# A second product of gate factors, moved in front of the scores of a unit

## The chip, the cores and the metric

The kernel runs on one core of one Trainium2 chip. The metric is the device time of one execution in microseconds (us); the median of three runs is 523.07 us, the lowest 521.63 and the highest 526.06. Unless a unit is named, times are microseconds from the start of the profiled execution's span.

## The reference, cut to what matters

The input goes through a gated linear attention with exponential gates and then through a mixture of experts. For each step `t` of each of 4 x 8 sequences (768 steps, 40 wide):

```
m_new  = max(f + m, i)
f_stab = exp(f + m - m_new);  i_stab = exp(i - m_new)
C = f_stab * C + i_stab * outer(v, k);   n = f_stab * n + i_stab * k
y = sigmoid(o_gate) * (C q) / max(|n q|, 1)
```

The 3072 rows of `y` (320 wide) are then routed: logits plus a softplus-scaled noise, the best two of 8 experts for each row, and for each expert `relu(x w1) w2` weighted and added into the output.

## The kernel before, in words

The steps are cut into chunks of 64. A *unit* is one chunk of two of the four batches, that is 128 rows, with all 8 heads; there are 24 units. A written-out loop (`while i < NU - LEAD`, L792) runs 22 iterations, 0 to 21; each handles parts of several units, since the parts of one unit are spread over successive iterations. The instructions of each engine run in the order in which the loop issues them; no planner reorders them, and every engine waits only for the data and the buffers that its next instruction needs.

What an iteration `i` puts on the engines, in the order of the code:

- **k_part, p_part** (VectorE): the keys and the scores of unit `i+1` are multiplied by its gate factors `W` (L350, L356).
- **c_part, o_part** (TensorE): the state update of unit `i` into the bank `st` (L370), its copies on ScalarE (L373), and the output of unit `i` into the bank `o` (L379).
- **e_part** (TensorE, then ScalarE): the *gate factors* of unit `i+2`. A product of 98 rows and 512 columns (L318) gives the exponents of one of the two batches; ScalarE takes their exponential into `W` (L321). `p` = 0 is the first product, `p` = 1 the second. Both go into the one bank named `e`, so that the second product has to wait until the exponential of the first has read the bank.
- **f_part** (VectorE, GpSimd): normalizes the output of unit `i` and multiplies it with the sigmoid of its output gate (L384 to L391).
- **l_part, r_part, b_part** (TensorE): router logits of unit `i-2` (L422), in some iterations ranks (L431 to L433) or a *burst* of products that builds the table of rows (L442).
- **t_part, tc_part**: transposes of unit `i-1` on TensorE (L402), their copy on ScalarE (L406). **lc_part, bc_part** copy logits, ranks and burst out of the bank (L471, L474, L451).
- **s_part** (TensorE): the scores of unit `i+2`, 8 products of 64 x 64 x 256 (L339) and 32 of 64 x 64 x 64 (L342), which work in quarters of the array.
- **sig_part** (ScalarE): the sigmoid of the output gate of unit `i+1`, three instructions in place (L326 to L328).
- **act** issues small exponentials and logarithms of the router on ScalarE when they are due (L685); **fill** issues router work on VectorE up to a budget.

In even iterations from 8 on, ScalarE and GpSimd also split a piece of the first expert's weights (L150). The weights, queries and values arrive over DMA queues that the SyncE engine issues; GpSimd issues the writes of the finished rows. After the loop the last two units are finished by hand, and the experts follow, from about 126 us to the end.

Of the kernel before, what the change touches and what calls it, by code (L numbers as in the profile page):

```python
# [41 lines left out]
LEAD = 2  # L42
# [19 lines left out]
def build(ctx, tc, qk, vk, fi, noise, wgn, w1, w2, cst, ce, out):  # L62
# [59 lines left out]
    def piece_w1(e, f, k):  # L122
        c = slice(f, f + 512)
        if k < 2:
            SP.dma_start(RAW1[:, k, c], w1[e, 128 * k:128 * k + 128, c])
        else:
            for p in range(2):
                SP.dma_start(RAW1[64 * p:64 * p + 64, 2, c], w1[e, 256:320, c])
# [25 lines left out]
    def load_unit(u, what="kv", q=None):  # L154
        pr, c = divmod(u, NCH)
        if "k" in what:
            for n in (slice(0, 32), slice(32, D)):
                for p in range(2):
                    (q or SP).dma_start(QK[u % 4][64 * p + n.start:64 * p + n.stop], qk[pr, c, p, n])
        if "v" in what:  # L160
            flat = VKS[u % 4].rearrange("p x c -> p (x c)")
            SP.dma_start(flat[0:64, 0:VW], vk[pr, c, 0])
            SP.dma_start(flat[64:128, 648:648 + VW], vk[pr, c, 1])
# [59 lines left out]
    def gate_move(kk, q=(SP, SP)):  # L223
        pr, k = divmod(kk, GB)
        j = kk % 2
        src = HL[32 * pr:32 * pr + 32, :, k * GC * L:(k + 1) * GC * L].bitcast(F32)
        q[0].dma_start(LE[j][64:96, :, 64:128].bitcast(F32), src[:, 0].rearrange("r (c t) -> r c t", c=GC))
        q[1].dma_start(RE[j][96:98].bitcast(F32), src[:, 1])
# [43 lines left out]
    def gate_steps(n):  # L272
        for _ in range(n):
            next(gates2, None)
# [9 lines left out]
    def constants():  # L284
        P.memset(W1L[0:64, 2].bitcast(F32), 0.0)
        P.memset(zrow, 0.0)
        P.memset(TBL, 0.0)
        P.memset(WTS, 0.0)
# [23 lines left out]
    def e_part(u, ps_=(0, 1), first=False):  # L312
        pr, c = divmod(u, NCH)
        j = (GB * pr + c // GC) % 2
        c = c % GC
        for p in ps_:
            ps = XTB if first and p else psum.tile([128, 512], F32, name="e")
            T.matmul(ps, LE[j][0:KE, c, 64 - 64 * p:192 - 64 * p], RE[j][0:KE, p, :, c * L:c * L + L], start=True, stop=True)  # L318
            if p == 0:
                W[u] = wk.tile([128, 2, H, L], F32, name="w", bufs=LEAD)  # L320
            A.activation(W[u][:, p].rearrange("p h t -> p (h t)"), ps, AF.Exp)  # L321

    def sig_part(u):

        g = SG[u % 4]
        A.activation(g, g, AF.Exp, scale=-1.0)  # L326
        A.activation(g, g, AF.Ln, bias=1.0)
        A.activation(g, g, AF.Exp, scale=-1.0)  # L328
# [4 lines left out]
    def s_part(u):  # L333
        q = QK[u % 4]
        for h in range(H):
            if whole(u) and h % 4 == 0:
                for p in range(2):
                    r = qrow[p]
                    T.matmul(SQ[u][:, p][r][:, h:h + 4, :], ident[r, r], q[r, 0, h:h + 4, :], start=True, stop=True)  # L339
            for p in range(2):  # L340
                r = qrow[p]
                T.matmul(SQ[u][:, p][half[p], h, :], q[r, 1, h, :], q[r, 0, h, :], start=True, stop=True)  # L342

    def whole(u):
        return u % NCH > 0

    def k_part(u):
        if u % NCH < NCH - 1:
            KD[u] = wk.tile([128, 2, H, D], F32, name="kd")
            V.tensor_mul(KD[u], VKS[u % 4][:, :, 328:648].rearrange("p x (h d) -> p x h d", h=H),  # L350
                         W[u][:, :, :, L - 1:L].to_broadcast([128, 2, H, D]))

    def p_part(u):
        PP[u] = wk.tile([128, 2, H, L], F32, name="p")
        if whole(u):
            V.tensor_mul(PP[u], SQ[u], W[u])  # L356
        else:
            for p in range(2):
                n = half[p]
                V.tensor_mul(PP[u][n, p], SQ[u][n, p], W[u][n, p])  # L360
# [32 lines left out]
    def keep_rows(u):  # L393
        (P if u < XV - 1 else SP).dma_start(XD[128 * u:128 * u + 128, 0:DM], XR[u])
# [50 lines left out]
    def bc_part(t, b, late=False):  # L445
        if b:
            s = late or rt.tile([128, NE * TC], F32, name="share", bufs=2)
            if late:
                V.tensor_add(TBL, TBL, t[:, LGC + 24:LGC + 24 + NE * TC])
            else:  # L450
                A.activation(s, t[:, LGC + 24:LGC + 24 + NE * TC], AF.Copy)  # L451
                P.tensor_add(TBL, TBL, s)
            done[0] += len(b[0]) // 2

    def decode(a, b):

        t, n = TBL[:, a:b], slice(a, b)
        V.scalar_tensor_tensor(VC[:, n], t, 0.0, cs[:, C_VAC + a:C_VAC + b], op0=OP.is_equal, op1=OP.mult)
        V.tensor_scalar(AB[:, n], t.bitcast(I32), 16, 0x7fff, op0=OP.arith_shift_right, op1=OP.bitwise_and)
        V.tensor_scalar(KM[:, n, 0], t, 0.0, None, op0=OP.is_gt)  # L460
        V.scalar_tensor_tensor(TOK[:, n], AB[:, n], -float(CODE), VC[:, n], op0=OP.add, op1=OP.add)
        V.tensor_scalar(KM[:, n, 1], t, 0.0, None, op0=OP.is_lt)
# [282 lines left out]
    def gather(e, h=None, ts=None):  # L745

        for t in ts or tiles(e, h):

            n = NTOK if h is None else 128 * E0U[h]
            P.indirect_dma_start(out=XG[0:rows_of(e, t), t], out_offset=None, in_=XD[0:n],  # L750
                                 in_offset=bass.IndirectOffsetOnAxis(ap=token(e, t), axis=0),
                                 bounds_check=n - 1, oob_is_err=False)
# [3 lines left out]
    def early_w2(j, n):  # L756

        SP.dma_start(raw2[:, j:j + n], w2[0, 128 * j:128 * (j + n)].rearrange("(j p) c -> p j c", p=128))
# [8 lines left out]
    def tiles(e, h=None):  # L767
        if h is None:
            return range(6 + (CAPS[e] > NM))
        c = parts(e)[h]  # L770
        return range(c.start // 128, -(-c.stop // 128))
# [19 lines left out]
    i = 0  # L791
    while i < NU - LEAD:  # L792
        unit[0] = i
        spent[0] = 0.0
        while sent:
            SP.dma_start(*sent.pop())
        if 1 <= i and i + 3 < NU:
            load_unit(i + 3)
        if i:
            keep_rows(i - 1)  # L800
        if i % 2 == 0 and i and i // 2 + 2 < 2 * GB:
            gate_move(i // 2 + 2, (P, P) if i < XV else (SP, SP))

        if W1LD <= i < W1LD + 12 and i % 2 == 0:
            j = (i - W1LD) // 2
            piece_w1(0, 512 * (j // 3), j % 3)
        if i == W2AT:
            early_w2(0, 2)
        if i == 3:
            SP.dma_start(cs[:, C_TRI:], cst[:, C_TRI:])  # L810
        if i == 4:
            SP.dma_start(nzt, noise)
        if not begun and done[0] >= E0U[0]:
            decode(0, E0S[1] // 128)
            spent[0] += 0.6
            begun = 1
        if begun and late < len(tiles(0, 0)):
            gather(0, 0, tiles(0, 0)[late:late + 2])
            late += 2
            begun = 2  # L820
        if i == 6:
            constants()
            A.activation(tri, cs[:, C_TRI:C_TRI + 128], AF.Copy)
            A.activation(ones, cs[:, C_ONE:C_ONE + 128], AF.Copy)
            A.activation(iob, cs[:, C_N:C_N + 128], AF.Copy)
        k_part(i + 1)
        p_part(i + 1)
        fill(0.2, False)
        s_room(i + 2)
        c_part(i)  # L830
        o_room(i)
        o_part(i)
        e_part(i + LEAD, (0,))
        if i == 0:
            sig_part(0)
        f_part(i, lambda: fill(0.15, False))
        if i < 2:
            gate_steps(4)
        if i == 0:
            gate_move(2, (P, P))  # L840
        t = l_part(i)
        w = r_part(t)
        b = None if w else b_part(t)
        if i:
            t_part(i - 1)
            tc_part(i - 1)
        lc_part(i, t, w)
        bc_part(t, b)
        s_part(i + 2)
        act()  # L850
        if i:
            sig_part(i + 1)
        e_part(i + LEAD, (1,))
        if i == 0:
            sig_part(1)
        route(i)
        fill((SHARE if i < NU - 3 else 0.8) - spent[0])
        if W1AT <= i < W1AT + 12 and i % 2 == 0:
            next(pre1)
        act()  # L860
        if 0 < i < 7:
            gate_steps(4)
        if 6 <= i < 13:
            P.memset(XG[:, i - 6], 0.0)
        i += 1
# [482 lines left out]
```

## Time and profile before

| | before |
|---|---|
| median of three runs | 523.07 us |
| profiled execution, its own time | 522.65 us |
| span of the profiled execution | 520.9 us |
| TensorE busy, share of the span | 504.6 us, 97% |
| VectorE, ScalarE, GpSimd busy | 341.3, 248.7, 243.3 us |
| mean granted TensorE clock | 0.985 |

The profile shows one execution. PE is the matmul side of TensorE, PEld its weight loads, DVE is VectorE, ACT is ScalarE, POOL is GpSimd, SP is SyncE. A row of a timeline gives the start, the duration, the engine, the line, the operation and the tiles written and read; a number in brackets at its end is the idle time of the engine ahead of it and what ended that. Rows with a count merge several instructions. Durations of matmuls contain their way through the array, so that the spacing of their starts, not their duration, says what they cost the engine.

### The profile page before, as it was taken

Reading aid. Unit: us, or ns where it says so; the run is one execution under the profiler, and the core shown is the slowest. Engines: PE = TensorE matmul, PEld = TensorE weight load, DVE = VectorE, ACT = ScalarE, POOL = GpSimd, SP = SyncE. Lnnn points to the kernel's source line nnn. Section 1 sums busy time; section 2 is a strip of 40 time slices with the busy share of each in tenths; the row PEclk is TensorE's granted clock in tenths of the full one; section 3 lists DMA queues with packets and bytes.
Section 4 is the critical chain, followed back from the end, with each engine's and each line's share of the span. In section 5 each row is a group of like instructions: output and inputs, shape, how many; then the busy total and the mean of one; then the engine's idle time right before and its main releaser. Section 6 shows DMA issues by size and latency. Waiting matters only on the chain.

```text
span 520.9 us, 13365 instructions
## 1 busy us (share of the span) xinstructions
PE 504.6 (97%) x5130; PEld 473.3 (91%) x5130; DVE 341.3 (66%) x905; ACT 248.7 (48%) x594; POOL 243.3 (47%) x321
## 2 busy tenths in 40 slices
PE   8899999999999999999999999999999999999993
PEld 3788888888889988999999999999999999999993
DVE  6899998986997576763865484377548347546310
ACT  5788879978523255441542354054335325515300
POOL 7545686864543846055415614550562254151033
PEclk9799999999989999999999999999999999999998
DMA  5889999986655848079229516832951683272033
GB/s 153 201 217 243 246 242 248 223 235 207 216 195 165 202 57 213 5 163 234 68 53 274 112 28 139 229 91 48 263 99 51 138 221 88 60 169 26 2 40 41
DMA packets 48955, 76.89 MB, mean 148 GB/s; under 512 B 10645, under 2 KB 37980, under 8 KB 48884
## 3 DMA queue, kind: packets, MB, share of 16 engines
q1 hardware_dynamic: 35668, 52.19, 36.3%
q0 software_dynamic: 11616, 20.57, 20.7%
q10 hardware_dynamic: 1600, 3.21, 2.0%
q8 instruction: 42, 0.69, 0.6%
q14 instruction: 29, 0.24, 0.2%
HBM read 52.42 MB, written 17.40 MB: 134 GB/s over the span
## 4 chain that ended last, share of the span: by engine, by line
PE 66%; DMA 13%; DVE 11%; ACT 3%; issue 2%; POOL 2%; SPq 1%; POOLq 0%; DVEq 0%; ACTq 0%
PE s L981 16%; DMA y_out<-y,tok 9%; PE e L981 8%; PE o L1009 4%; PE o L1008 4%; PE o L1007 4%; PE st L1008 4%; PE st L1009 4%; PE st L1007 4%; PE o L379 4%; PE e L318 3%; PE s L342 2%; DVE hlo L993 2%; PE st L370 2%; DMA qk<-qk_in 2%
## 5 line engine op out<-in xcount | busy, mean ns | idle before, releaser
L1035 POOL DMA_INDIRECT y_out<-y,tok x53 | 87.2, 1645 | 184.8 <-DVE y L1025 182.0
L992 ACT ACTIVATE hh<-s 128x384 fp32r<-128x384 f32 (+3 forms) x91 | 42.6, 470 | 83.8 <-PE s L981 82.7
L981 PE MATMUL s<-xh,w1h 128*128 128x384 f32 (+6 forms) x273 | 76.8, 337 | 0.1
L750 POOL DMA_INDIRECT xg<-rows,tok x53 | 57.3, 1082 | 24.6 <-issue 15.5
L993 DVE SCALAR_TENSOR_TENSOR hlo<-s,hh 128x384 fp32r<-128x384 f32 (+3 forms) x91 | 47.6, 523 | 24.9 <-ACT hh L992 24.3
L981 PE MATMUL s<-xh,w1l 128*128 128x384 f32 (+6 forms) x273 | 61.7, 334 | 0.0
L1009 PE MATMUL o<-w2h,hlo 128*128 128x320 f32 x184 | 56.9, 309 | 0.7 <-DVE hlo L993 0.7
L1008 PE MATMUL o<-w2l,hh 128*128 128x320 f32 x184 | 56.8, 309 | 0.0
L1007 PE MATMUL o<-w2h,hh 128*128 128x320 f32 x184 | 56.3, 306 | 0.2 <-ACT hh L992 0.2
L1009 PE MATMUL st<-w2h,hlo 128*128 128x320 f32 x168 | 51.9, 309 | 0.0
L1008 PE MATMUL st<-w2l,hh 128*128 128x320 f32 x168 | 51.8, 308 | 0.0
L1007 PE MATMUL st<-w2h,hh 128*128 128x320 f32 x168 | 51.2, 305 | 0.0
L981 PEld LDWEIGHTS s<-xh,w1h 128*128 128x128 f32 x273 | 49.2, 188 | 1.5 <-ACT xh L782 0.4
L981 PEld LDWEIGHTS s<-xh,w1l 128*128 128x128 f32 x273 | 47.7, 188 | 1.1 <-DVE xh L784 0.2
L981 PE MATMUL s<-xl,w1h 128*128 128x384 f32 (+6 forms) x182 | 46.1, 334 | 0.3 <-DVE xl L783 0.3
L992 ACT ACTIVATE hh<-e 128x384 fp32r<-128x384 f32 (+3 forms) x45 | 21.3, 473 | 49.3 <-PE e L981 49.3
L981 PE MATMUL e<-xh,w1h 128*128 128x384 f32 (+6 forms) x135 | 38.6, 340 | 0.6 <-DVE hlo L993 0.3
L1025 DVE TENSOR_SCALAR y<-o,gw 128x320 f32<-128x320 f32 x22 | 12.1, 550 | 39.9 <-PE o L1009 39.9
L391 POOL TENSOR_TENSOR xr<-tm,vk 128x320 f32<-128x320 f32 x24 | 21.1, 879 | 34.7 <-DVE tm L390 13.6
L1025 DVE TENSOR_SCALAR y<-st,gw 128x320 f32<-128x320 f32 x20 | 11.0, 550 | 39.3 <-PE st L1009 39.3
L1009 PEld LDWEIGHTS o<-w2h,hlo 128*128 128x128 f32 x184 | 34.5, 188 | 0.9 <-DVE hlo L993 0.9
L1007 PEld LDWEIGHTS o<-w2h,hh 128*128 128x128 f32 x184 | 34.5, 188 | 0.6 <-ACT hh L992 0.4
(237 smaller groups left out, 1290.7 us busy)
## 6 DMA issues: line engine op xcount, KB each, us to landing
vk<-vk_in SPq DMA_DIRECT2D x48, 242.0 KB
raw<-w_in SPq DMA_DIRECT2D x6, 1280.0 KB
raw<-w_in SPq DMA_DIRECT2D x6, 1024.0 KB
qk<-qk_in SPq DMA_DIRECT2D x46, 128.0 KB
y_out<-zrow SPq DMA_DIRECT2D x15, 320.0 KB
raw<-w_in SPq DMA_DIRECT2D x16, 256.0 KB
rows<-xr POOLq DMA_DIRECT2D x23, 160.0 KB, 4.3
xt__2801<-xb SPq DMA_DIRECT2D x40, 72.0 KB
```

Of the source, the lines that this page charges most:

```text
L318: T.matmul(ps, LE[j][0:KE, c, 64 - 64 * p:192 - 64 * p], RE[j][0:KE, p, :, c * L:c * L + L], start=True, stop=True)
L379: T.matmul(OQ[u][half[p], h, :], PP[u][n, p, h, :], VK[u % 4][p][n, h * 41:h * 41 + 41], start=True, stop=True)
L391: P.tensor_mul(XR[u], tm.rearrange("p h d -> p (h d)"), SG[u % 4])
L750: P.indirect_dma_start(out=XG[0:rows_of(e, t), t], out_offset=None, in_=XD[0:n], in_offset=bass.IndirectOffsetOnAxis(ap=token(e, t), axis= ...
L981: T.matmul(ps[:, 0:n], l, r, start=i == 0, stop=i == len(ops) - 1)
L992: A.activation(hi, x, AF.Relu)
L993: V.scalar_tensor_tensor(lo, x, 0.0, hi.bitcast(F32), op0=OP.max, op1=OP.subtract)
L1007: T.matmul(ps, HH[:, j, c], W2H[:, j], start=j == 0, stop=False)
L1008: T.matmul(ps, HH[:, j, c], W2L[:, j], start=False, stop=False)
L1009: T.matmul(ps, HLO[:, j, c], W2H[:, j], start=False, stop=j == 7)
L1025: V.tensor_scalar(y[0:n], ps[0:n], GW[e][0:n, t:t + 1], None, op0=OP.mult)
L1035: st = P.indirect_dma_start(out=out, out_offset=bass.IndirectOffsetOnAxis(ap=token(e, t), axis=0), in_=y[0:n], in_offset=None, compute_op= ...
```

## The change

In iterations 1 to 21 the second product of gate factors of unit `i+2` and its exponential are issued behind the copies of logits and transposes and in front of the scores `s_part`; so the product stands on TensorE between the transposes and the scores, and the exponential on ScalarE in front of `act` and of the three instructions of the sigmoid. In iteration 0 the order stays as it was.

```
         lc_part(i, t, w)
         bc_part(t, b)
+        if i:
+            e_part(i + LEAD, (1,))
         s_part(i + 2)
         act()
-        if i:
-            sig_part(i + 1)
-        e_part(i + LEAD, (1,))
         if i == 0:
-            sig_part(1)
+            e_part(LEAD, (1,))
+        sig_part(i + 1)
         route(i)
```

## Rows read from the trace of the kernel before

**Rows 1.** Windows view, stretches 27 to 48 and 79 to 113 us: busy us by engine, clock, DMA.

```profile
27.00:48.00 21.00, 20.88 (x526) 18.15 (x527) 19.78 (x42) 17.52 (x43) 8.57 (x14) 1.00 0.88 226
79.00:113.00 34.00, 33.47 (x817) 28.92 (x816) 30.12 (x90) 29.92 (x76) 24.22 (x37) 1.00 0.95 234
```

**Rows 2.** Timeline of TensorE's matmuls, iteration 13 of the loop (start us, us).

```profile
81.42 0.50 PE L318 MATMUL e<-re,le 98*128 98x512 f32 x1
81.75 0.74 PE L422 MATMUL xt<-wgt,xts 128*128 128x16 f32 x6
82.34 0.53 PE L402 MATMUL xt<-cs,xr 128*128 128x128 f32 x3
82.80 0.43 PE L339 MATMUL s<-qk,cs 64*64 64x256 f32 x2
...
83.89 0.51 PE L318 MATMUL e<-re,le 98*128 98x512 f32 x1
84.33 0.82 PE L370 MATMUL st<-vk,kd 104*40 104x41 f32 x32
...
86.01 0.49 PE L318 MATMUL e<-re,le 98*128 98x512 f32 x1
```

**Rows 3.** Timeline of TensorE: transposes with a whole-array product behind them.

```profile
129.95 0.52 PE L402 MATMUL xt<-cs,xr 128*128 128x128 f32 x3
130.23 0.60 PE L981 MATMUL s<-xh,w1h 128*128 128x384 f32 x2
```

**Rows 4.** Timeline of TensorE, iteration 0, a stretch at half clock.

```profile
19.22 0.79 PE L318 MATMUL e<-re,le 98*128 98x512 f32 x1
19.94 0.69 PE L339 MATMUL s<-qk,cs 64*64 64x256 f32 x2
...
21.86 0.79 PE L318 MATMUL e<-re,le 98*128 98x512 f32 x1
22.58 1.32 PE L370 MATMUL st<-vk,kd 104*40 104x41 f32 x32
```

**Rows 5.** Timeline of ScalarE, iteration 13.

```profile
81.95 0.60 ACT L321 ACTIVATE w<-e 128x512 f32<-128x512 f32 x1
82.91 0.49 ACT L406 ACTIVATE xts<-xt 128x384 f32<-128x384 f32 x1 [0.35 <-PE xt L402]
...
84.74 0.58 ACT L321 ACTIVATE w<-e 128x512 f32<-128x512 f32 x1
```

**Rows 6.** Timeline, all engines: a product of factors that waited for its bank.

```profile
69.85 0.58 ACT L321 ACTIVATE w<-e 128x512 f32<-128x512 f32 x1
...
70.48 0.19 PEld L318 LDWEIGHTS e<-re,le 98*128 98x128 f32 x1 [0.16 <-ACT w L321]
```

**Rows 7.** Timelines of TensorE and ScalarE: late first exponentials, iterations 8 and 14.

```profile
57.18 0.50 PE L318 MATMUL e<-re,le 98*128 98x512 f32 x1
...
58.00 0.58 ACT L321 ACTIVATE w<-e 128x512 f32<-128x512 f32 x1
...
86.81 0.58 ACT L321 ACTIVATE w<-e 128x512 f32<-128x512 f32 x1
```

**Rows 8.** Timelines of TensorE and ScalarE, iteration 1.

```profile
25.31 0.49 PE L402 MATMUL xt<-cs,xr 128*128 128x128 f32 x3
...
25.50 0.60 ACT L321 ACTIVATE w<-e 128x512 f32<-128x512 f32 x1
```

**Rows 9.** Timeline of VectorE, iterations 3 and 4.

```profile
34.33 0.79 DVE L350 TENSOR_TENSOR kd<-vk,w 128x640 f32<-128x640 f32 x1
...
39.06 0.81 DVE L350 TENSOR_TENSOR kd<-vk,w 128x640 f32<-128x640 f32 x1
```

**Rows 10.** Waits between engines, 17 to 126 us (total us, times, longest us).

```profile
DVE kd L350 <- ACT w L321: 5.1, 5, 2.4
```

**Rows 11.** Timelines of VectorE and TensorE: the burst of iteration 18.

```profile
103.19 2.87 DVE L615 TENSOR_SCALAR ob<-iob,bi,cs 128x128 bf16<-128x128 bf16 x10
...
105.41 0.91 PE L442 MATMUL xt<-oa,ob 128*128 128x56 bf16 x12
```

## The prediction

> **What bounds the kernel now.** I first read the windows view. In the loop TensorE is busy without a gap that matters, 33.47 of 34.00 us between 79 and 113 us, at the full granted clock of 1.00; VectorE (30.12), ScalarE (29.92) and the DMA engines (share 0.95) are close behind it. Between 27 and 48 us VectorE is nearer to full than later (19.78 of 21.00) [rows 1]. A busy matmul row does not say what is lost between two kinds of products, so I read TensorE's timeline next, by the spacing of starts. Iteration 13 takes 86.01 - 81.42 = 4.59 us from first product of factors to first product [rows 2]. In it the transposes stand for 0.46 us before the scores start (82.80 - 82.34), and the second product for 0.44 before the state update starts (84.33 - 83.89), while the first, with the logits behind it, stands for only 0.33 (81.75 - 81.42) [rows 2]. The difference is what follows: a product in pieces of the array (scores, state) costs its predecessor more than one that uses the whole array. The same three transposes with a whole-array product behind them take 130.23 - 129.95 = 0.28 us [rows 3].
>
> So the change, which only reorders, does touch TensorE's path: it takes away one passage from whole-array work to scores (the transposes') and turns the passage scores to product to state into product to scores to state.
>
> **The change part by part, TensorE.** Nothing is added or removed; the 21 products, 21 exponentials and 63 sigmoid instructions of iterations 1 to 21 stay, and the moved step issues no DMA.
>
> Transposes to product: 0.28 instead of 0.46, so -0.18 us. Product to scores: not in the trace at full clock. At half clock, product to scores is 19.94 - 19.22 = 0.72 and product to state 22.58 - 21.86 = 0.72, equal [rows 4], so I take the 0.44 that product to state costs now: no difference. Scores to state: nowhere in the trace. Now scores to product is 83.89 - 82.80 = 1.09 [rows 2]. It may cost more by the 0.11 that a passage to pieces costs over one to whole-array work (0.44 - 0.33), and less by at most the 0.19 of a whole weight load of the product [rows 6]. I take 1.09, since the 40 score products in it are the same, and keep -0.19 and +0.11 for the range. Sum for an undisturbed iteration: 0.28 + 0.44 + 1.09 = 1.81 against 0.46 + 1.09 + 0.44 = 1.99, or -0.18 us.
>
> **The new wait.** The second product needs the bank that the first exponential reads, and now it comes 0.28 us after the transposes' start instead of behind the scores. In iteration 13 the exponential runs from 81.95 to 82.55 [rows 5]; a product that waits for its bank starts its load 0.05 us after the exponential's end (69.85 + 0.58 = 70.43, load at 70.48) [rows 6]. So it could start at 82.60, and TensorE reaches it at 82.34 + 0.28 = 82.62, or 1.20 after the first product. There is no slack, but no loss. What queues behind a late one is everything on TensorE: the scores and the next state update.
>
> ScalarE is late in some iterations, behind splits and router exponentials. In iteration 8 the product could start at 58.00 + 0.58 + 0.05 = 58.63, TensorE would be there at 57.18 + 1.20 = 58.38: 0.25 late, a net of +0.07. In iteration 14 it is 86.81 + 0.63 = 87.44 against 87.21: 0.23 late, net +0.05 [rows 2, 7]. These are the two worst that I saw among iterations 7 to 21; three more (9, 15, 17) lie between them and iteration 13, and I count them at the middle, -0.06 each. The other ten are clean. Iterations 7 to 21: 10 x 0.18 + 3 x 0.06 - 0.07 - 0.05 = 1.86 us gained.
>
> Iteration 1 has no logits, which brings the product closer to its predecessor: it could start at 25.50 + 0.60 + 0.05 = 26.15, and TensorE is there at 25.31 + 0.28 = 25.59 [rows 8]. The wait of 0.56 less 0.18 costs 0.38. That is hidden, and so is any gain of iterations 2 to 6: there VectorE, with its gate steps, sets a period of 39.06 - 34.33 = 4.73 us [rows 9] against TensorE's 4.59, which leaves TensorE 5 x 0.14 = 0.7 us. If VectorE did not pace those, the 0.38 would show and five more gains of 0.18 with it. I count both at nothing.
>
> **ScalarE and VectorE.** In iteration 13 the second exponential goes from 84.74 to behind the copy of the transposes, which ends at 82.91 + 0.49 = 83.40 [rows 5]: 1.3 us earlier. By then its product (82.62, with a duration of 0.51) is done, so ScalarE does not wait. The sigmoid moves back by the one exponential's 0.6 us; GpSimd uses it only an iteration later, so nothing follows. Who gains is VectorE, which stood 5.1 us in five places for that exponential [rows 10]. It is not the bound there, so those 5.1 us are no gain by themselves; they let VectorE run ahead of the two bursts. That matters, because the burst of iteration 18 ends at 105.41 + 0.91 = 106.32, shortly behind VectorE's last operand at 103.19 + 2.87 = 106.06 [rows 11]. What TensorE gains in iterations 13 to 17 (0.18 - 0.05 + 0.06 + 0.18 + 0.06 = 0.43), and in 7 to 11 ahead of the first burst (0.18 - 0.07 + 0.06 + 0.18 + 0.18 = 0.53), survives only if VectorE is earlier too. I keep half of this 0.96.
>
> **Sum.** 1.86 - 0.48 = 1.4 us, carried to the end, since the experts' part is TensorE's. Against the profiled execution, 522.65 - 1.4 = 521.25; that execution is 0.42 under the median of 523.07, so on the scale of the runs 521.7.
>
> **The rivals.**
>
> *No change: another engine paces the loop.* VectorE at 30.12 and the DMA engines at 0.95 of 34 us [rows 1] leave little to follow with, and any earlier TensorE then waits at a burst or for a load. For it: rows 11; against it: TensorE's own 33.47. Time 523.1.
>
> *Slower: ScalarE's lag decides.* ScalarE is busy 29.92 of 34 us and stands a further 0.35 us in each iteration until the transposes are done [rows 1, 5]; at 34 / 4.59 = 7.4 iterations that is 2.6, together 32.5. Gaining 0.18 per iteration leaves 34 - 1.3 = 32.7, so it is about full, and its first exponential may slip in every iteration as it does in 8 and 14. The place is the bank of the two products; the point is a first exponential that starts more than 0.53 + 0.18 = 0.71 us after its product (0.53 is iteration 13's). With twice the lag of iteration 8 in all fifteen, 15 x (0.50 - 0.18) = 4.8 us, 527.9; with half as much again, 15 x (0.38 - 0.18) = 3.0, 526.1. [...] Against it: lags push themselves out, since a TensorE that waits gives ScalarE time. I put it at 525.5.
>
> *Faster than forecast: the product's weights are in place before it may start.* In the row that shows a product waiting for its bank, the load itself started after the exponential, 0.19 us long [rows 6]. Were it done under the transposes, up to 0.19 more would go in each of fifteen iterations: 2.9 on top of 1.86, 518.3. The same size would come from a cheap passage from scores to state (the -0.19 above). [...]
>
> **How the numbers follow.** Forecast 0.50, no change 0.27, slower 0.15, faster still 0.08. The time is the forecast's, 521.7. Its own bounds are wide: scores to state at +0.11 in fifteen iterations is +1.65, which turns it into no change; at -0.19 it is the third rival; and three runs of one kernel spread from 521.63 to 526.06. The range 519.4 to 524.4 holds most of the first two cases and some of each of the others, about 8 in 10. A measurement can tell about 1%, 5.2 us, from no change. Faster than 517.8 needs the third rival and the gains of iterations 2 to 6 on top: 0.04. Slower than 528.3 needs more than the dear end of the second: 0.03. Within: 0.93.
>
> **What would show it.** Right: transposes to second product about 0.28, product to scores about 0.44, scores to state about 1.1; an undisturbed iteration of 4.4 us; VectorE's waits for the second exponential far below 5.1 us; the loop ending 1 to 2 us earlier. Wrong: weight loads of the second product idle behind the first exponential by more than 0.2 us in most iterations (slower), or a loop that ends when it did, with TensorE waiting for VectorE or loads instead (no change).

## The result and the profile after

| | before | after |
|---|---|---|
| median of 19 runs each, same chip | 522.87 us (519.93 to 526.45) | 527.37 us (522.17 to 532.94) |
| ratio | | 1.0067, 95% interval 1.0042 to 1.0092 |
| profiled execution, its own time | 522.65 us | 523.21 us |
| span; TensorE busy | 520.9; 504.6 us | 521.3; 499.0 us |

The kernel became 0.67% slower, about 3.5 us. I had forecast 521.7 and nothing above 524.4. The profiled execution of after is one of the fastest of its 19 runs, so the pair of profiles differs by 0.6 us where the medians differ by 4.5: most of the loss has to be looked for in further executions, as is done below. The ratio, unlike the medians, leaves out three runs of after (530.1 to 532.9 us) as disturbed. The 0.6 us are there when the experts begin: their first product starts at 130.82 us, against 130.23 before [rows 3], and from there to the end it is 390.5 and 390.7 us.

The windows view of after, the same stretches as [rows 1] (columns: TensorE matmul, weight loads, VectorE, ScalarE, GpSimd busy us; granted clock; DMA share; GB/s):

```profile
27.00:48.00 21.00, 18.66 (x398) 16.41 (x396) 19.54 (x40) 14.16 (x34) 8.63 (x13) 0.89 0.95 234
79.00:113.00 34.00, 33.40 (x838) 29.62 (x837) 31.37 (x90) 29.66 (x75) 23.98 (x37) 1.00 0.96 242
```

In the second stretch after runs 838 matmuls where before ran 817, at the same busy time: here the new order is faster. In the first it ran 398 against 526, and the granted clock is 0.89.

The timeline of TensorE, iteration 13, to be laid beside [rows 2]:

```profile
83.73 0.50 PE L318 MATMUL e<-re,le 98*128 98x512 f32 x1
84.07 0.74 PE L422 MATMUL xt<-wgt,xts 128*128 128x16 f32 x6
84.65 0.52 PE L402 MATMUL xt<-cs,xr 128*128 128x128 f32 x3
84.93 0.48 PE L318 MATMUL e<-re,le 98*128 98x512 f32 x1
85.35 0.43 PE L339 MATMUL s<-qk,cs 64*64 64x256 f32 x2
...
86.44 0.82 PE L370 MATMUL st<-vk,kd 104*40 104x41 f32 x32
...
88.12 0.49 PE L318 MATMUL e<-re,le 98*128 98x512 f32 x1
```

Transposes to product 0.28, product to scores 0.42, scores to state 1.09, one iteration 4.39 instead of 4.59 us. The waits of other engines on the new place, after, 17 to 126 us (total us, times, longest us):

```profile
PEld e L318 <- ACT w L321: 2.8, 4, 1.6
DVE kd L350 <- ACT w L321: 2.5, 2, 1.4
...
PE o L379 <- issue: 1.9, 1, 1.9
PE e L318 <- ACT w L321: 1.7, 3, 1.3
```

VectorE's stand for the second exponential fell from 5.1 [rows 10] to 2.5 us. So the mechanism of the gain is there. Where the time went shows in the spacing of first products, after and then before:

```profile
18.14 0.50 PE L318 MATMUL e<-re,le 98*128 98x512 f32 x1
...
36.79 0.50 PE L318 MATMUL e<-re,le 98*128 98x512 f32 x1
...
55.37 0.50 PE L318 MATMUL e<-re,le 98*128 98x512 f32 x1
...
121.77 0.50 PE L318 MATMUL e<-re,le 98*128 98x512 f32 x1
```

```profile
38.58 0.50 PE L318 MATMUL e<-re,le 98*128 98x512 f32 x1
...
52.61 0.50 PE L318 MATMUL e<-re,le 98*128 98x512 f32 x1
...
120.64 0.50 PE L318 MATMUL e<-re,le 98*128 98x512 f32 x1
```

These are iterations 0 (after only; before it is 19.22 [rows 4]), 4, 7 and 21. From 0 to 4 after takes 18.65 us against 19.36. That is not the order's doing: before ran from 17.39 to 24.22 us at half clock [rows 4], and after did not; the old order of h1 (below), which like after is at full clock there, takes 18.64 (first products at 17.55 and 36.19). From 7 to 21 it is 66.40 against 68.03, a gain of 1.63 (I had 1.86 less half of 0.96). But from 4 to 7 it takes 18.58 against 14.03: 4.55 us lost in three iterations. TensorE's timeline there, iteration 5, and the windows before and behind the stand:

```profile
40.48 0.90 PE L379 MATMUL o<-vk,p 104*64 104x41 f32 x24 [0.16 <-DVE tm L390]
43.23 0.43 PE L379 MATMUL o<-vk,p 104*64 104x41 f32 x8 [1.86 <-issue]
43.60 0.80 PE L318 MATMUL e<-re,le 98*128 98x512 f32 x1
...
50.98 0.50 PE L318 MATMUL e<-re,le 98*128 98x512 f32 x1
```

```profile
36.00:43.40 7.40, 5.38 (x143) 4.77 (x139) 7.09 (x14) 4.92 (x12) 3.87 (x6) 1.00 1.02 241
43.50:50.30 6.80, 6.80 (x103) 6.10 (x101) 5.33 (x10) 3.98 (x12) 4.02 (x8) 0.50 0.93 248
```

TensorE stands 1.86 us in the middle of 32 like products, and "issue" says that the profile shows no semaphore, no buffer and no other engine that held it. Right behind the stand the granted clock is 0.50 from 43.50 to 50.30 us; the product of factors there takes 0.80 instead of 0.50, and the way from iteration 5's first product to iteration 6's (43.60 to 50.98), in which the profile shows no wait of TensorE's products, 7.38 us instead of the 4.39 from there to iteration 7's (50.98 to 55.37): 2.99 more. The stand's 1.86 and these 2.99, less three gains of 0.19, make 4.3, against the 4.55 lost.

**What the stand is.** The page's table of DMA queues has a row that I had passed over; before and after have it alike:

```profile
q8 instruction: 42, 0.69, 0.6%
```

42 packets of 16,384 bytes each, which I read as TensorE's program arriving while it runs; the page counts them against the same 16 DMA engines as the loads. The trace has 10,402 TensorE instructions, 248 for each packet, and the stands listed here, and every one above 0.6 us that the rows below put down to "issue", come at a TensorE instruction whose number is 193 modulo 256. Counted out of the trace (times in us; "asked" is when TensorE reached the boundary before, since no row shows the request itself):

```
kernel             number  asked   packet           goes on  stand
before              1985    48.19   50.21 -  51.23    53.99   none
before              4801   106.64  109.67 - 110.94   112.52   0.45
before              5313   117.92  121.12 - 122.16   123.68   0.62
after               1473    36.10   40.43 -  41.78    43.23   1.86
after, again (e1)   3777    86.50   92.23 -  93.38    94.95   3.05
after, again (h4)   1729    41.60   44.86 -  45.96    47.47   0.59
after, again (h4)   2241    54.20   57.40 -  58.46    59.88   0.53
```

In the loops of before and after a boundary comes every 4.7 to 6 us where no stand and no half clock lies between. The packet for the next 256 instructions starts after the boundary before; where that takes 1 to 2 us (the first row), it has landed with time to spare. In the other rows it starts 3 us or more late; there TensorE goes on 1.4 to 1.6 us after the packet has landed, and stands until then. A late packet need not cost anything: behind after's stand the next one started 3.6 us late too and had landed at 47.99, but TensorE, at half clock, came to it only at 51.34. While the packet of number 1473 waits the DMA engines are full: share 1.02 in the window above. The kernel before had such stands too, "PE s L342 <- issue: 1.0, 2, 0.6" in its own waits, and I read over it.

### The profile page after: what moved, and what is told of

The parts are those of the page before. It is cut to its first block, busy times and chain, and to the rows that moved or that the text cites. A ratio compares the mean times of both kernels' runs of the same rounds, so it can differ in the third digit from the quotient of the medians.

```text
span 521.3 us, 13367 instructions
## 1 busy us (share of the span) xinstructions
PE 499.0 (96%) x5130; PEld 470.9 (90%) x5130; DVE 343.2 (66%) x905; ACT 248.0 (48%) x594; POOL 242.4 (47%) x321
## 4 chain that ended last, share of the span: by engine, by line
PE 60%; DMA 14%; DVE 11%; ACT 7%; issue 3%; SPq 2%; POOL 1%; POOLq 0%; DVEq 0%; ACTq 0%
PE s L981 16%; DMA y_out<-y,tok 9%; PE e L981 8%; PE o L1009 4%; PE o L1008 4%; PE o L1007 4%; PE st L1009 4%; PE st L1008 4%; PE st L1007 4%; PE o L379 3%; DVE hlo L993 3%; DMA qk<-qk_in 2%; PE e L318 2%; PE s L342 2%; DVE w2l L764 1%
```

## The experiments

Each kernel is timed against the kernel before on the same chip; chips differ (before: 523 to 530 us), so kernels are compared within a group.

**First group: where in the loop does it lose?** The rivals then were waits of the first iterations (EARLY) and ScalarE's lag throughout (LAG). The kernels differ in the one condition under which the new place holds, `i > 0` (e1, the change as it is), `i > 1` (e2), `i > 6` (e3), `0 < i < 7` (e4). e3, against before, cut to the new place:

```
+        moved = i > 6
+        if moved:
+            e_part(i + LEAD, (1,))
...
+        if not moved:
             e_part(i + LEAD, (1,))
```

e1: 

> The changed kernel once more, for a second trace and a time beside the variants. Theory EARLY: the loss is made in iterations 1 to 6, where the second product waits for ScalarE (1.34 us in iteration 1 of the changed kernel's trace) and where a stall of TensorE or a stretch at half clock can follow; iterations 7 to 21 gain 1.5 to 2 us as forecast. It expects a ratio to the kernel before of 1.005 to 1.009, and in the trace a distance from the first product of iteration 7 to that of iteration 21 near 66.4 us, against 68.0 before. Theory LAG: the product waits for a late ScalarE all along the loop; it expects the same ratio, with waits of the product above 0.2 us in most of iterations 7 to 21 and no gain in that distance.

e2: 

> New order from iteration 2 on; iteration 1 keeps the old one. EARLY, if the wait of iteration 1 is the cause: the loss is gone, ratio 0.996 to 1.000. LAG: the loss stays, 1.005 or more. If something else in iterations 2 to 6 is the cause, the loss stays too, and the next run is without it.

e3: 

> New order in iterations 7 to 21 alone. EARLY: ratio 0.996 to 0.999, some 1 to 2 us faster than the kernel before. LAG: 1.004 or more, since most of the waits stay.

e4: 

> New order in iterations 1 to 6 alone. EARLY: the whole loss and none of the gain, ratio 1.008 to 1.012. LAG: a third of the loss at most, 1.000 to 1.003.

Measured against before: e1 531.66 us, 1.0069 [1.0001, 1.0138]; e2 530.08, 1.0045 [0.9978, 1.0111]; e3 531.59, 1.0066 [1.0001, 1.0131]; e4 530.61, 1.0056 [0.9995, 1.0117]. EARLY's 0.996 to 0.999 for e3 lies outside its interval; that either part of the loop alone loses is likely, but the intervals are too wide to show it. The trace of e1 tells what to look for: from iteration 7 to 21 it takes 75.5 us, where EARLY had 66.4, and no second product there waits more than 0.2 us for ScalarE, where LAG had most of them. TensorE's timeline and two windows (the first from boundary to packet, the second behind the stand):

```profile
90.85 1.04 PE L379 MATMUL o<-vk,p 128*64 128x41 f32 x29
94.95 0.31 PE L379 MATMUL o<-vk,p 104*64 104x41 f32 x3 [3.06 <-issue]
```

```profile
86.50:92.20 5.70, 5.21 (x134) 4.44 (x130) 5.55 (x16) 5.37 (x16) 3.37 (x6) 1.00 0.99 264
...
95.20:102.00 6.80, 6.80 (x102) 6.15 (x101) 4.70 (x22) 3.59 (x10) 3.26 (x7) 0.50 0.92 238
```

The same picture as after's iteration 5, in another iteration and larger: for 5.7 us the DMA engines are full at 0.99 and the code packet does not start, TensorE stands 3 us, and the clock is at 0.50 behind it. EARLY and LAG both fall as the main cause, and a third theory takes their place.

**Second group: code packets behind the loads, or the order itself?** FETCH: the stands come from code packets delayed by a full DMA. ORDER: the new order loses by its own waits. f1 (old order) and f2 (new) load less:

```
-        if "v" in what:
+        if "v" in what and u < 4:
```

f1: 

> The old order, with the values, keys and output gates loaded for units 0 to 3 only; later units read the same four buffers again, so about half of the bytes of the loop's loads and none of its engine work is left out. FETCH (TensorE's code comes in 16,384-byte packets over the same loaded DMA engines, and where such a packet starts late TensorE stands; in the new order it stands more often and longer): the code packets start soon after they are asked for, no stand of over 0.3 us at an instruction number of 193 modulo 256 in the loop, 0.5 to 4 us faster than the kernel before (0.992 to 0.999). ORDER (the new order is slower because of its own waits for ScalarE, whatever the loads do): within 0.998 to 1.002 of the kernel before, as no engine's work has changed.

f2: 

> The new order, with the same loads left out as in the run beside it. FETCH: with the loads out of the way the gain of about 0.19 us in each iteration comes through to the end: 1.5 to 3.5 us faster than the old order with these loads left out (ratio between the two 0.993 to 0.997), no long stand at an instruction number of 193 modulo 256, half clock no more often than in the old order. ORDER: it is slower than the old order with these loads left out, by the same 2 to 4 us as with all loads (ratio 1.003 to 1.009).

f3 (new order) doubles a product, f4 (old order) drops one:

```
-            T.matmul(ps, LE[j]..., RE[j]..., start=True, stop=True)
+            for _ in range(1 + (p == 1 and u > LEAD)):
+                T.matmul(ps, LE[j]..., RE[j]..., start=True, stop=True)
```

```
-            for j in range(3):
-                T.matmul(t[:, LGC:LGC + 16], ..., start=(j == 0), stop=(j == 2))
+            for j in range(2):
+                T.matmul(t[:, LGC:LGC + 16], ..., start=(j == 0), stop=(j == 1))
```

f3: 

> The new order, in which from unit 2 on the second product of gate factors is issued twice into the same place (2 instructions and about 0.22 us of TensorE more in each of 18 or so iterations; its exponential starts that much later). FETCH: code is asked for as often in time, since instructions and time grow together; TensorE is nearer to its old pace of 4.6 us an iteration and stands less often, so the time is that of the changed kernel or lower (1.000 to 1.006 of the kernel before). ORDER: 18 times 0.2 us come on top of what the changed kernel lost: 1.010 to 1.016.

f4: 

> The old order, with the third of the three matmuls of the router's logits left out (the logits lack the last columns), which takes 2 to 4 instructions and about 0.19 us off TensorE's part of each iteration, as the new order does, but without touching the order of products, scores and exponentials. FETCH: a TensorE that is faster by this little gains nothing at the end, because it meets its code sooner: 0.998 to 1.008 of the kernel before, with stands and half clock in the loop as in the changed kernel. ORDER: only the new order loses, so this one shows the whole 3 to 4 us (0.992 to 0.995).

Measured: f1 521.41 us, 0.9973 [0.9950, 0.9995]; f2 519.96, 0.9936 [0.9908, 0.9965]; f3 529.58, 1.0122 [1.0077, 1.0167]; f4 522.33, 0.9977 [0.9950, 1.0004].

The pair f1 and f2 is the clearest of the study: with the DMA engines half empty (shares of 0.46 and 0.48) the sign turns, new to old 0.9936 / 0.9973 = 0.9963, by medians 1.45 us faster, about the gain forecast (the interval of that ratio, worked out below, ends at 1.000). The mean clock of their runs is equal, 0.991 and 0.991. From 25 to 125 us, f1 and then f2, and f2's waits of TensorE for ScalarE:

```profile
25.00:125.00 100.00, 98.55 (x2401) 85.33 (x2401) 88.34 (x231) 84.45 (x211) 64.50 (x100) 1.00 0.46 141
```

```profile
25.00:125.00 100.00, 95.81 (x2384) 85.18 (x2382) 90.55 (x234) 84.09 (x210) 64.03 (x102) 1.00 0.48 142
```

```profile
PE e L318 <- ACT w L321: 1.7, 3, 1.3
...
PE s L342 <- issue: 0.9, 1, 0.9
PE o L379 <- issue: 0.8, 1, 0.8
```

f2 has the same 1.7 us of waits for ScalarE as after, and wins. So ScalarE's lag is not what costs, and ORDER falls as the whole cause. The two waits on "issue" are a miss for FETCH, which expected no long stand in f2: they are stands for code, of 0.76 and 0.88 us (numbers 1473 and 4801), behind packets that started 3.4 and 3.8 us late; f1 has none. No half clock follows them. On average over the loop the packets start 0.8 us late in f1, 1.6 in f2, 1.8 in before and 2.0 in after: with half the loads the new order still has its code late. A third packet shows that full DMA engines are not the only reason; it started 3.2 us late (number 1729) while their share was 0.25:

```profile
41.60:44.80 3.20, 3.15 (x63) 2.74 (x64) 3.03 (x7) 1.90 (x5) 0.21 (x1) 1.00 0.25 92
```

But FETCH in the form in which I had put it falls too. It said that TensorE meets its code sooner because it is faster. f3 is back at the old pace (4.63 us in undisturbed iterations) and should have been no slower than after; it came out at 1.0122, where ORDER had it. Its profile, of its slowest run, has the longest stand of all:

```profile
96.39 0.64 PE L380 MATMUL o<-vk,p 128*64 128x41 f32 x15
101.35 0.87 PE L380 MATMUL o<-vk,p 128*64 128x41 f32 x12 [4.33 <-issue]
```

That is number 3777 again, asked at 91.86, its packet from 98.46 to 99.73. Against the order alone (1.0067 to 1.0083) that is 2 to 3 us more, for about 4 us of added work. Its interval is 2.4 us wide to either side, and work in this loop need not show in full at the end (f4, next), so f3 does not tell how much of the loss the slower pace took away; its profile shows that it did not end the stands. f4 makes TensorE faster by as much as the change does (4.37 us in undisturbed iterations), without touching the order of the products. Some 20 x 0.2 = 4 us of work gained 1.2 at the end (0.0023 of 523, 2.6 at most by the interval), a value between both expectations: a gain of TensorE's in this loop is passed on in part. Its profile has the stands that FETCH expected, in the old order: the longest is 1.89 us, at number 5313 (asked at 119.39, packet from 123.70), and behind it 31 products of L379 take 1.93 us, where 32 take 1.13 from 130.56 on.

**Third group: take traffic away or add it, with the result unchanged.** g1 (new order) and g2 (old) load expert 0's first weights as whole rows (and split them two iterations later); g3 (new) asks for values an iteration later; g4 (old) adds a load:

```
-            SP.dma_start(RAW1[:, k, c], w1[e, 128 * k:128 * k + 128, c])
+        SP.dma_start(RAW1[64 * x:64 * x + 64, k], w1[e, n:n + 64])
```

```
+            load_unit(i + 2, "v")
...
-            load_unit(i + 3)
+            load_unit(i + 3, "k")
```

```
             SP.dma_start(flat[64:128, 648:648 + VW], vk[pr, c, 1])
+            if u > 3:
+                SP.dma_start(flat[64:96, 648:648 + VW], vk[pr, c, 1, 0:32])
```

g1: 

> The new order, with expert 0's first weights loaded in the loop as whole rows of 4,096 bytes, 64 rows every second iteration from 6 to 16 and split two iterations later (a packet of 2,048 bytes took about 166 ns of a DMA engine and one of 4,096 bytes 234 ns in the trace of the changed kernel, so the same bytes take some 2 us less of all 16 engines over these iterations). TRAFFIC (what delays TensorE's code packets, and with them the new order, is the bytes queued ahead of them): a part of the loss comes back, 1.000 to 1.005 of the kernel before, a higher mean clock than the changed kernel's. ORDER (the new order's own waits for ScalarE): nothing changes, 1.005 to 1.009.

g2: 

> The old order with the same whole rows. TRAFFIC: a little faster than the kernel before, 0.996 to 1.000, as stands and half clock grow rarer. ORDER: as the kernel before, 0.999 to 1.001.

g3: 

> The new order, with the values, keys and output gates of a unit asked for one iteration later than its queries (the same bytes, in two smaller bursts, and less far ahead). TRAFFIC: fewer bytes are queued ahead of a code packet, the longest start delays fall below 4 us and the time to 1.000 to 1.005 of the kernel before; if instead the data itself comes late, TensorE waits for it at the transposed keys and products, and the time is above 1.007. ORDER: 1.005 to 1.009.

g4: 

> The old order, with 32 rows of each unit's values, keys and gates from unit 4 on read a second time into the same place (124 KB, about 0.5 us of all 16 DMA engines more in an iteration; no engine work is changed). TRAFFIC: code packets start later, TensorE stands at instruction numbers of 193 modulo 256 and falls to half clock more often: 1.005 to 1.015, at a lower mean clock. ORDER: the loads have slack, 0.999 to 1.003.

Measured: g1 533.07 us, 1.0070 [1.0035, 1.0104]; g2 526.96, 0.9970 [0.9931, 1.0010]; g3 533.55, 1.0082 [1.0043, 1.0120]; g4 578.04, 1.0913 [1.0858, 1.0967]. g1 and g3 are misses for TRAFFIC, and their times lie where ORDER had them: a small thinning and a different spacing did not bring the new order back. g2 fits both theories. g3's waits show that its stands remained:

```profile
PE o L379 <- issue: 5.0, 4, 1.9
PE st L370 <- issue: 1.0, 2, 0.5
PE e L318 <- ACT w L321: 0.8, 2, 0.7
```

g4 went far beyond its 1.015, by another mechanism, which its waits of SyncE's queue and of TensorE tell (30 to 135 us):

```profile
SPq L165 <- DMA vk<-vk_in: 48.1, 13, 4.7
```

```profile
PE s L341 <- DMA qk<-qk_in: 17.0, 7, 5.0
```

The second load writes where the first one writes, and SyncE's queue waited 48.1 us in all for loads of values to land, so that the queries behind them came late. It says nothing on code packets; it shows only how much a blocked load queue costs (its mean granted clock was 0.93).

**Fourth group: the middle dose, and traffic that nobody reads.** h1 (old) and h2 (new) load the values of even units only, h3 (old) reads 16 rows into a spare tile, h4 is the change again:

```
-        if "v" in what:
+        if "v" in what and (u < 4 or u % 2 == 0):
```

```
+            if u > 3:
+                SP.dma_start(SPARE[u % 2], vk[pr, c, 1, 0:16])
```

h1: 

> The old order, with values, keys and gates loaded for units 0 to 3 and the even units only; odd units read the buffer as it is (about a fifth of the loop's bytes left out, half of what the lighter pair left out). CODE (TensorE's code packets wait behind the loads; what they cost depends on how full the DMA engines are): 0.996 to 1.000 of the kernel before. ORDER (the waits for ScalarE): 0.998 to 1.002.

h2: 

> The new order with the same loads left out. CODE: between the pair with all loads (ratio of new to old 1.0067) and the lighter pair (0.996): new to old 0.997 to 1.003, and the longest start delay of a code packet in the loop below that of the full kernel in the new order. ORDER: new to old as with all loads, 1.004 to 1.009.

h3: 

> The old order with all its loads, and 16 rows of each unit's values from unit 4 on read once more into a spare place that nothing reads (62 KB, about 0.25 us of all 16 DMA engines an iteration; one more transfer of some 0.5 us in the queue of SyncE). CODE: the loop's transfers still fit, but code packets start later: 1.003 to 1.010, with stands of TensorE and half clock as the new order has them. ORDER: nobody waits for these bytes, 0.999 to 1.002.

h4: 

> The new order once more with all loads, so that the pairs stand on one chip: 1.004 to 1.009 by CODE and by ORDER alike; the trace should again show stands at instruction numbers of 193 modulo 256 behind code packets that start 3 us or more after they are asked for.

Measured: h1 527.90 us, 0.9984 [0.9943, 1.0026]; h2 526.68, 1.0031 [0.9995, 1.0067]; h3 531.25, 1.0088 [1.0052, 1.0125]; h4 530.94, 1.0083 [1.0040, 1.0125]. DMA shares of 25 to 125 us are the last but one number of the windows, here h2 and h4:

```profile
25.00:125.00 100.00, 96.17 (x2394) 84.96 (x2391) 88.27 (x231) 83.65 (x207) 63.88 (x100) 1.00 0.70 191
```

```profile
25.00:125.00 100.00, 95.58 (x2393) 84.22 (x2394) 86.83 (x227) 83.34 (x207) 63.54 (x100) 1.00 0.95 243
```

| loads | DMA share of the new order's profile | new to old |
|---|---|---|
| all (h4) | 0.95 | 1.0083 [1.0040, 1.0125] |
| even units' values (h2 to h1) | 0.70 | 1.0031 / 0.9984 = 1.0047 [0.999, 1.010] |
| four units' values (f2 to f1) | 0.48 | 0.9936 / 0.9973 = 0.9963 [0.993, 1.000] |

The last two intervals are worked out from those of the two ratios as if these were independent. The ratios fall with the load, as the theory of code packets (CODE) says, but the middle one is 0.002 above what I expected and within ORDER's 1.004 to 1.009, and the medians of that pair say the opposite (526.68 against 527.90): it is inconclusive. h3 is not. With 62 KB an iteration that no instruction reads, the old order becomes as slow as the new one. Its window, the stand and its waits (17 to 126 us):

```profile
25.00:125.00 100.00, 94.70 (x2285) 81.70 (x2285) 84.00 (x226) 82.11 (x202) 63.43 (x99) 1.00 0.98 241
```

```profile
126.14 0.33 PE L345 MATMUL s<-qk 64*64 64x64 f32 x5 [1.97 <-issue]
```

```profile
PE e L321 <- DMA re<-hl: 1.8, 1, 1.8
PE s L342 <- DMA qk<-qk_in: 1.4, 4, 0.7
PE st L373 <- issue: 0.9, 2, 0.4
```

So with a DMA share of 0.98 TensorE stands 2.0 us for code (number 5313, asked at 118.89, packet from 123.16), and 3.2 us for data that came late. ORDER's 0.999 to 1.002 is excluded: traffic alone can cost this kernel as much as the new order does. That it costs it through code is shown for a part only. On average over the loop h3's packets start no later than before's (1.65 against 1.81 us; the latest 4.28 against 3.20), and the late data are the larger part of its stands. h4's waits for comparison:

```profile
PE st L370 <- issue: 0.9, 2, 0.5
PE e L318 <- ACT w L321: 0.9, 2, 0.7
PE s L342 <- issue: 0.8, 2, 0.5
...
PE xt L422 <- issue: 0.6, 1, 0.6
```

The one at L422 and the longer one at L342 are the two of h4 in the list above, behind packets that started 3.2 to 3.3 us after they were asked for, as expected. But h4's profile, of its fastest run, does not show the loss: its experts begin at 129.29 us, earlier than before's on the first chip (130.23), and it is their part that is longer, 396.9 us. On this chip that part takes 393.7 to 396.9 us in either order, on the first and on that of the second group 390.2 to 390.7, so this is not the order's. The pair at the state update (L370), of 0.45 us each, stands elsewhere; h3 and g3 have it too, and its cause was not looked for.

**How much of it is the clock.** On h4's chip the mean granted clock is 0.9813 over 10 runs of the new order and 0.9854 over the 30 of before that its ratio counts. At the level of 0.50 that the profiles show, 0.0041 x 2 x 525 = 4.3 us more of each run lie at half clock; at the rate of after's iteration 5, 2.99 us lost in 6.8, that takes TensorE some 1.9 us, an estimate. The means of the times differ by 531.3 - 526.9 = 4.4. The rest, 2.5 us, and the 1.5 to 1.9 us that the order gains, are what stands at full clock eat, as an estimate.

No run was faster than both kernels with the result kept: g2 is the nearest, within its interval of before.

## Why the prediction was wrong, point by point

- **Transposes to product, product to scores, scores to state.** Right: 0.28, 0.42 and 1.09 us against 0.28, 0.44 and 1.09. An undisturbed iteration is 4.39 us, as forecast; none of the bounds -0.19 and +0.11 was needed.
- **The new wait.** Right. In iteration 8 of after the product stands 0.18 us for its bank, and its weight load indeed waits with it:

```profile
61.40 0.50 PE L318 MATMUL e<-re,le 98*128 98x512 f32 x1 [0.18 <-ACT w L321]
```

```profile
61.40 0.19 PEld L318 LDWEIGHTS e<-re,le 98*128 98x128 f32 x1 [0.42 <-ACT w L321]
```

  So what the third rival needs, weights in place ahead of a product that waits, does not hold in that row, nor in after's three other waits of that kind, in which the load stands 0.37 to 1.57 us. Iteration 1 was under-priced: the product waited 1.34 us, not 0.56. I had read the 0.56 from an execution whose iteration 0 ran at half clock; after's ran at full clock, so that TensorE came to the transposes at 22.12 instead of 25.31 us, while ScalarE still had three sigmoids and the copies of the state (L373) in front of the first exponential. That the wait stays hidden was right: with it, iterations 0 to 4 take as long in after (18.65 us) as in h1 with the old order (18.64).

```profile
23.95 0.50 PE L318 MATMUL e<-re,le 98*128 98x512 f32 x1 [1.34 <-ACT w L321]
```

- **VectorE.** Right in direction: its stand fell to 2.5 us, and in this pair of profiles iterations 7 to 21 kept 1.63 of 1.86 us, more than the 1.4 that I let stand.
- **"1.86 - 0.48 = 1.4 us, carried to the end, since the experts' part is TensorE's."** This is the step that failed. The gain is there in the iterations and in the pair f1 and f2, but with all loads it does not reach the end. I took TensorE for bound by its own work, and had nothing in the sum for the delivery of its program and for half clock behind a stand. In after's profile one stand of 1.86 us for code and the 6.8 us at half clock behind it turned three iterations' gain into a loss of 4.55, against 1.63 gained in fourteen. The program is delivered while the DMA engines are at a share of 0.95, which I had in [rows 1] and read only as a pace that leaves little to follow with, not as a queue in which TensorE's code may stand. That code stands also make the larger loss of the other executions is argued from the profiles of e1, f3 and g3, not shown run by run.
- **The rivals.** "ScalarE's lag decides" named a time near the result (525.5) for a reason that was not the one: its place, the bank of the two products, cost 1.7 us in after, 1.34 of it in iteration 1, and the same 1.7 us in f2, which is faster than its partner. "Another engine paces the loop" was nearest in naming the DMA engines, but it could only return the gain, not turn it into a loss. No case was there for a stand with half clock behind it, and the range ended at 524.4.
- **What stays open.** Why the code packets start late more often in the new order than in the old at the same traffic and, in f3, at the same pace. In all ten profiles with the new order in iterations 4 to 7 one of the numbers 1473, 1729 and 1985 starts over 3 us late, in four of the eight with the old order there; number 3777 (about the end of iteration 14) does in five of ten and in none of eight. The moment at which they are asked for may fall into full stretches of the loads, but f2 has the lateness at half the loads too; so the full DMA engines are a condition that was varied, and the link from the order to the late packets is not shown. Whole rows (g1) and a later request (g3), meant to empty the queue there, did not help.

## What to carry to other kernels

Look at the bounding engine's waits that nothing explains ("issue") and at the DMA queue of kind "instruction" before banking a gain: here a program of some ten thousand TensorE instructions came in beside the loads, and its packets could come late, in both orders at DMA shares of 0.92 to 0.98 and in the new one even at 0.48. Price a stand of TensorE at full clock by its length and by what the clock does behind it, from rows; here 1.86 us of standing cost some 4.9, with the 3.0 of the clock. Before comparing stretches of two profiles, look at the clock in both. And where a change of a few us is at stake, do not read it from one pair of profiles: these two differed by 0.6 us, the medians by 4.5.

## What the runs showed of the hardware that was not expected

- What I read as TensorE's code comes in packets of 16,384 bytes, 42 in before and in after, one packet ahead: in the loops of all profiles a packet started after the boundary before was reached, but for three in f1 and h4 that started up to 0.6 us ahead of it. Behind the stands of 0.45 us and more listed above TensorE went on 1.4 to 1.6 us after the packet had landed, in before, after, e1, f3, h3 and h4 alike; the packet itself took about 0.9 to 1.5 us in most cases and 2.0 at most.
- Half clock came right behind two stands of TensorE: from 43.55 us behind one of 1.86 that ended at 43.23 (after), from 95.20 behind one of 3.06 that ended at 94.95 (e1). Behind the stands of 0.5 to 0.6 us in h4's list and the two of f2 it did not come. In before's and after's profiles no wait of TensorE's products from 160 to 260 us is over 0.7 us; in e1, h3 and h4 they also stand 2.1 to 2.3 us in the experts, in either order (until 186.25 in e1, 178.90 in h4):

```profile
178.90 0.74 PE L981 MATMUL e<-xh,w1h 128*128 128x192 f32 x2 [2.15 <-ACT xh L782]
```

  This is h4. It is one reason why times are compared within a group only.
